# Fixed slots for the pages, moved steps and a three-piece end in a fused Fourier-mixing and gated kernel

## The chip, the cores and the metric

The kernel runs on one core of a Trainium2 chip. The metric is the device time of one execution in microseconds, lower is better. Before the change the median of 3 runs is 802.62 us (801.09 to 804.1).

## The reference

Everything is float32, with S = 2048 positions, D = 512 channels and F = 1792 hidden units.

```python
x = A_x
xn = _layernorm(x, axis=-1)
s = _A_ref(xn, A_dft_seq_re, A_dft_seq_im, A_dft_hid_re, A_dft_hid_im)
g = _silu(_B_ref(xn, B_w_gate, B_w_up, B_w_down))
return x + s * g
```

`_A_ref` multiplies xn by the real and imaginary hidden matrices (512 x 512) to get a and b, then by the sequence matrices (2048 x 2048), and returns Cr a - Ci b. `_B_ref` computes h = sigmoid(xn Wg) * (xn Wu) and returns h Wdown.

## The kernel before

**Products.** Each large product is cut into two-by-two blocks and done in seven block products instead of eight, so that each needs sums and differences of blocks first (`combine`, L128, on VectorE, DVE) and joins of partial results afterwards. Each operand is split into a high part, copied by ScalarE (ACT, L72), and a low part, its difference from the input, by DVE (L73). `mm3` (L75 to L78) then does three matmuls: high x high, high x low, low x high.

**Pages.** All operands, sums and snapshots lie in pages of 4 KB a partition. `page` (L45) asks a pool of 54 slots (`PAGES`, L26) for one, and the pool picks the slot. Whoever first writes a new page waits until everything that read or wrote the slot's former page is done: SyncE (SP) when it is a load (L87, L759), ACT or DVE when it is a split or a sum.

**Order.** The program is a list of units, each with its operands (`needs`) and a function that issues its matmuls. The loop at L1145 walks through it: first come the steps that were placed at this unit by `sooner`, then the loads of the next five units (`LOAD_AHEAD`), then the splits of the next two (`SPLIT_AHEAD`, three for units in `deep`), then the unit itself and the steps placed by `after`. So each engine's order is written out by hand, and each engine works its own queue in that order.

**Stages.** (1) `start` (L495) normalizes and transposes x, and begins the first gate block. (2) Thirteen `block`s (L432) do gate, up and sigmoid for a half of the positions and a group of hidden units; the down products of a block (`Seven`, L359) run during the next one and are added to g_part in HBM by stores from GpSimd (POOL, L312, L315). (3) `seq_units` (L930) multiplies the sequence matrices by xn in four chunks. `PLAN` (L705) writes each chunk's units as a string: a digit is a unit of product 1 to 7 (12 matmuls), a letter a unit of the inner products of a pair of chunks (6 matmuls). In each chunk product 1, 6, 7 and 4 use the chain "a" of two PSUM banks (ga and ua for chunks 0 and 1, gb and ub for 2 and 3, by `LETTER`), 2 the chain "b", 5 and 3 the chain "c" (`CHAIN`, L781). At the end of a product `done` copies a bank pair into a page (`snap`, L809, on ACT) or adds it to one (`join`, L816, on DVE), and `put` (L833) stores it to f_part from POOL. The remaining down products of stage 2 are put between the units after which `LEFT` (L321) names them. (4) `hidden_units` (L962) multiplies by the hidden matrices in two pairs of chunks, applies SiLU to g, multiplies and adds to x in `out`: x is copied there beforehand (`put_x`, L983) and the products are added by POOL's stores.

**Where steps stand.** `CSUM` and `ISUM` say how many units ahead of its use a sum of sequence blocks is made (3 and 4 where nothing is listed), `DEEP` which units split three units ahead, `AL` how early a weight page is loaded and split. `SL`, `GL` and `SI` do the same for sums, splits and SiLU of stage 4, and `LATE`, `S0`, `H0`, `L4`, `S4`, `H4` for the down weights and hidden sums of stage 2.

**The end.** `run_last` (L1075) does the last product in four pieces of columns, d0 256, d1 320 (`CUT`), d0 256, d1 192. Each is multiplied by the gate (L1083), added to x (L1084) and stored; the last is stored in two halves by SP and ACT (L1089).

Of the kernel before, what the change touches and what calls it, by code (L numbers as in the profile page):

```python
# [15 lines left out]
P = 128  # L16
# [6 lines left out]
NT = S // 512  # L23
SB = 512
EPS = 1e-5
PAGES = 54  # L26
SCRATCH = 4096
BLOCKS = (*((0, g) for g in range(1, 7)), (1, 6), *((1, g) for g in range(6)))
FIRST_TURNED = 1, 6
SPLIT_AHEAD = 2  # L30
LOAD_AHEAD = 5


@with_exitstack
def fnet_glu_kernel(ctx: ExitStack, tc: tile.TileContext, x, x_t, c_re, c_im, w_h, w_gu, w_down, out):
# [2 lines left out]

    const = ctx.enter_context(tc.tile_pool(name="const", bufs=1))
    stat = ctx.enter_context(tc.tile_pool(name="stat", bufs=4))  # L40
    pages = ctx.enter_context(tc.tile_pool(name="pages", bufs=PAGES))
    dram = ctx.enter_context(tc.tile_pool(name="dram", bufs=1, space=bass.MemoryType.DRAM))
    banks = ctx.enter_context(tc.tile_pool(name="banks", bufs=1, space=PSUM))

    def page(shape, dtype=F32R):  # L45
        return pages.tile([P, *shape], dtype, name="page")

    def bank(tag):
        return banks.tile([P, 512], F32, name=tag, bufs=2 if tag == "pd" else 1)
# [267 lines left out]

    GATED = {(0, 0): 1, (0, 1): 2, (1, 0): 4, (1, 1): 3}
    SEVEN = (5, 3, 1, 2, 6, 7, 4)
    LATE = 4, 5, 6, 8  # L320
    LEFT = 2, 4, 6, 8, 10, 11, 13  # L321
    HEAD = {(1, 0): "g", (1, 1): "g n u0", (2, 0): "u2", (2, 1): "p1 d0 d1 u1 r", (3, 0): "p3 x1 g d2 u3", (3, 1): "X5 g x2"}
    S0 = 7, 10, 12, 11
    H0 = 8, 11, 13, 14
    L4 = 10, 10, 13, 19
    S4 = 7, 8, 9, 11
    H4 = 8, 10, 11, 12
    SEVEN_LAST = (1, 2, 6, 7, 4, 5, 3)
    waiting = []

# [101 lines left out]
    def block(h, w, made, before, job, late):  # L432

        s, ps = job.s, {}
        n = len(units)
        if not made:
            for i, v in zip((-3, -1, 1, 3), w["s"]):
                sooner(n + i, v.get)

        def snap(k):  # L440
            s[k] = page([2, SB], F32)
            for m, c in enumerate("gu"):
                nc.scalar.activation(s[k][:, m, :], ps[c + "a"], AF.Copy)

        def seed():

            for c in "gu":
                ps[c + "b"] = bank(c + "b")
                nc.scalar.activation(ps[c + "b"], ps[c + "a"], AF.Copy)

        def plus(k):
            for m, c in enumerate("gu"):
                nc.vector.tensor_add(s[k][:, m, :], s[k][:, m, :], ps[c + "c"])

        def gate(k, tag=None):
            if tag:
                s[k] = page([2, SB], F32)
            nc.scalar.activation(s[k][:, 0, :], ps["g" + tag] if tag else s[k][:, 0, :], AF.Sigmoid)

        def times(k, tag=None):  # L460
            nc.vector.tensor_mul(s[k][:, 0, :], s[k][:, 0, :], ps["u" + tag] if tag else s[k][:, 1, :])

        tail = {1: seed, 6: lambda: snap(2), 7: lambda: (snap(3), plus(3)), 3: lambda: plus(2)}
        CH = {1: "a", 5: "c", 2: "b", 6: "a", 7: "a", 4: "a", 3: "c"}

        def unit(k, d):
            first = k in (1, 5)
            for m, c in enumerate("gu"):
                tag = c + CH[k]
                if first:  # L470
                    ps[tag] = bank(tag)
                product(k, ps[tag], w, h, m, first)
            if k in tail:
                tail[k]()
            if d:
                d[0].run(d[1])
            if k in (2, 4):
                gate({2: 1, 4: 4}[k], CH[k])
            if k in (7, 3):
                gate({7: 3, 3: 2}[k])  # L480
            if k == 4:
                times(4, "a")

        for i, k in enumerate((1, 5, 2, 6, 7, 4, 3)):
            if i == 2:
                waiting.extend((before, d) for d in before.items)
            d = waiting.pop(0) if waiting and i in waiting[0][0].at else None
            add([xop[h, k], w[k]] + (d[0].needs(d[1]) if d else []), lambda k=k, d=d: unit(k, d))
        sooner(n + 3, lambda: times(1, "b"))
        sooner(n + 5, lambda: times(3))  # L490
        sooner(n + 7, lambda: times(2))
        job.spread(n, late)
        return job
# [200 lines left out]
    def a_operands():  # L694
# [8 lines left out]
        return ops  # L703

    PLAN = (  # L705
        "111155556666aa33337777b4b444",
        "11ee1f15fc5c5566663gg377773d3d4444",
        "111155556666a7a777b44b443e3e3f3f",
        "1ccg1g1d155d556666337777334444",
    )  # L710
    LETTER = "aabb"
    DEEP = {(0, 1, 3), (0, 5, 3), (0, 6, 3), (0, 7, 3), (0, 4, 3), (1, 1, 3), (1, 5, 3), (1, 7, 3), (1, 4, 3), (3, 6, 3), (2, 4, 0), (2, 6, 3), (3, 4, 1), (3, 7, 3), (0, 7, 1), (3, 7, 0), (2, 7, 2), (0, 6, 0)}
    CSUM = {(0, 7, 1): 5, (2, 6, 0): 4, (2, 6, 1): 5, (1, 6, 0): 2, (3, 4, 2): 3, (1, 5, 1): 5, (2, 6, 3): 3}
    ISUM = {(2, 5, 1): 5, (2, 6, 0): 2, (0, 7, 1): 4, (2, 7, 1): 5, (0, 5, 0): 4, (2, 7, 0): 6}
    AL = {(0, 4, 2): 6, (0, 7, 0): 4, (0, 3, 0): 6, (0, 3, 2): 6, (0, 1, 0): 3, (0, 6, 2): 5, (0, 7, 2): 3}
    INNER_A = 1, 2, 5, 6, 3, 7, 4
    TURNED = (1, 5, 6, 2, 7, 3, 4)

# [211 lines left out]
    def seq_units(job, c_sums):  # L930
        ops = a_operands()
        left = waiting + [(job, k) for k in SEVEN_LAST]
        n = len(units)
        after(n + 40, lambda: nc.scalar.activation(warm, mhalf, AF.Silu))
        for q in range(2):
            sooner(n - (5, 1)[q] - 4, ops[1, q].load)
            sooner(n - (5, 1)[q], ops[1, q].get)
        inner_a([n + i for i in (-45, -38, -37, -36, -34, -31, -27, -24, -16, -10, -4)])
        chunks = [Chunk(i, c_sums) for i in range(NT)]
        starts = []  # L940
        pair = None
        for tc_, plan in enumerate(PLAN):
            starts.append(len(units))
            c = chunks[tc_]
            done = dict.fromkeys(CHAIN, 0)
            for t in plan.replace(" ", ""):
                if t in "abcdefg":
                    if pair is None or pair.ended():
                        pair = Inner(*chunks[tc_ // 2 * 2 :][:2])
                    pair.step("abcdefg".index(t) + 1)  # L950
                    continue
                k = int(t)
                c.step(ops, k, done[k])
                done[k] += 1
                if left and sum(done.values()) in LEFT:
                    last_down(*left.pop(0))
        assert not left
        blocks = [Load(w_h[i, j], [4, D // 2]) for i in range(2) for j in range(2)]
        sums_ahead(diffs, blocks, w_part, [starts[2] + i for i in (2, 8, 11, 16)], 4)


    def hidden_units():  # L962
# [1 line left out]
        v1, v3, v2, v4 = (Load(w_part[i], [4, D // 2]) for i in range(4))  # L964
        a11, a12, a22 = (Load(w_h[i, j], [4, D // 2]) for i, j in ((0, 0), (0, 1), (1, 1)))
        w = {}
        WH = {1: n - 9, 5: n - 8, 6: n - 3}
        for k, v in {1: a11, 5: v1, 6: v2, 2: a12, 7: v3, 3: v4, 4: a22}.items():
            w[k] = Parts([v], v.load, [4, D // 2])
            if k in WH:  # L970
# [1 line left out]
                after(WH[k], w[k].get)  # L972
        CHAIN = {1: "a", 6: "a", 7: "a", 4: "a", 2: "b", 5: "c", 3: "c"}
        BLOCK = {3: (0, 1), 7: (1, 1), 2: (0, 0), 4: (1, 0)}
        LAST, CUT = (NT // 2 - 1, 4), 320

        def place_out(pair, i, t):
            v = out[i * D // 2 : (i + 1) * D // 2, (2 * pair + t) * SB : (2 * pair + t + 1) * SB]
# [10 lines left out]

            return Value([g], make)  # L990

        SI = {(0, 2): 4, (0, 7): 9, (0, 3): 10, (1, 7): 12, (1, 2): 3}
        SL = {(0, 6, 0): 4, (0, 6, 1): 5, (0, 7, 0): 5, (0, 7, 1): 6, (0, 5, 1): 7, (1, 5, 1): 2, (1, 7, 0): 2, (1, 4, 1): 4}
        GL = {(0, 5, 0): 3, (0, 5, 1): 3, (0, 6, 0): 3, (0, 6, 1): 3, (0, 2, 0): 3, (0, 2, 1): 3, (0, 7, 0): 3, (1, 2, 1): 3, (0, 7, 1): 4, (1, 3, 0): 4, (1, 6, 0): 2}
        for pair in range(NT // 2):
            hp = {}
            sums = {}
# [13 lines left out]
            ps, s = {}, {}  # L1011
            for i, k in enumerate(TURNED):
                if k in BLOCK and (pair, k) != LAST:
                    after(n - (88, 84, 79, 77, 72, 67, 60, 60, 56, 68, 64, 58, 54)[i + 6 * pair], lambda pair=pair, k=k: put_x(pair, *BLOCK[k]))

            tags = {"a": ("pd", "b")[pair], "b": "c", "c": "a"}

# [57 lines left out]
            def run_last(k=4, hp=hp, ps=ps, pair=pair, gl=gl, xl=xl):  # L1075
                i, t = BLOCK[k]
                g, xv, r = gl[i, t].get(), xl[i, t].load(), page([2, SB], F32)
                hv, wv = [hp[k, half].get() for half in range(2)], w[k].get()
                for d, at in ((0, slice(0, SB // 2)), (1, slice(0, CUT)), (0, slice(SB // 2, SB)), (1, slice(CUT, SB))):
                    for kt in range(4):  # L1080
                        ws = [v[:, kt, d * P : (d + 1) * P] for v in wv]
                        mm3(ps["a", d][:, at], ws, [v[:, kt % 2, at] for v in hv[kt // 2]], False, kt == 3, go_on=True)
# [1 line left out]
                    nc.vector.tensor_add(r[:, d, at], r[:, d, at], xv[:, d, at])  # L1084
                    row, col = (2 * i + d) * P, (2 * pair + t) * SB
                    to = out[row : row + P, col + at.start : col + at.stop]
                    if (d, at.stop) == (1, SB):
                        for q, rows in ((nc.sync, slice(0, P // 2)), (nc.scalar, slice(P // 2, P))):
                            q.dma_start(to[rows], r[rows, d, at])  # L1089
                    else:  # L1090
# [24 lines left out]
    with tc.manual_schedule():  # L1115
# [15 lines left out]
        n = turned_at  # L1131
        turned_half(12, 0, (n - 19, n - 19, n - 18, n - 12))
        turned_half(19, 1, (n - 12, n - 11, n - 5, n - 5))
        for k, i in {1: -7, 5: -2, 2: -2, 6: 1, 7: 4, 4: 4}.items():
            sooner(n + i, xop[1, k].get)
        for k, i in {1: -4, 2: 0, 3: 1, 4: 2}.items():
            sooner(n + i, lambda k=k: x_sum(1, k))
        xn_sums(0, [n + i for i in (4, 7, 9, 9)])
        xn_sums(1, [n + i for i in (16, 17, 23, 24)])
        c_sums = [Value([], None) for _ in range(4)]  # L1140
        sums_ahead(sums, c_blocks(0, 0), c_sums, [n + i for i in (31, 32, 37, 39)], 3)
        seq_units(job, c_sums)
        hidden_units()
        begin()
# [74 lines left out]
```

## Time and profile before

| | |
|---|---|
| median of 3 runs | 802.62 us (801.09 to 804.1) |
| profiled execution, its own time | 799.84 us |
| its span, first to last instruction | 798.1 us |
| granted TensorE clock, mean | 0.999 |
| data moved by DMA | 172.13 MB, 216 GB/s |

The page of the profile gives each engine's busy time with its share of the span. PE stands for TensorE's matmuls, PEld for its weight loads, which overlap them. A row of the timeline gives a start, a length, the engine, the line of the kernel, the operation, out<-in by tile names, the shape, and in brackets the idle time of that engine just before, with what ended it. The ends of matmuls are modelled, so the distance between two starts tells more of PE than busy time does.

### The profile page before, as it was taken

Reading aid. Unit: us, or ns where it says so; the run is one execution under the profiler, and the core shown is the slowest. Engines: PE = TensorE matmul, PEld = TensorE weight load, DVE = VectorE, ACT = ScalarE, POOL = GpSimd, SP = SyncE. Lnnn points to the kernel's source line nnn. Section 1 sums busy time; section 2 is a strip of 40 time slices with the busy share of each in tenths; the row PEclk is TensorE's granted clock in tenths of the full one; section 3 lists DMA queues with packets and bytes.
Section 4 is the critical chain, followed back from the end, with each engine's and each line's share of the span. In section 5 each row is a group of like instructions: output and inputs, shape, how many; then the busy total and the mean of one; then the engine's idle time right before and its main releaser. Section 6 shows DMA issues by size and latency. Waiting matters only on the chain.

```text
span 798.1 us, 10300 instructions
## 1 busy us (share of the span) xinstructions
PE 790.9 (99%) x3600; PEld 657.7 (82%) x3600; DVE 710.4 (89%) x931; ACT 540.2 (68%) x840; POOL 123.7 (16%) x169
## 2 busy tenths in 40 slices
PE   9999999999999999999999999999999999999997
PEld 7988888888888888888888877888888888888886
DVE  6999899899998989889998887989879899978986
ACT  4688888888877878878977746554444545548371
POOL 2004351111221222112110000000200000000102
PEclk9999999999999999999999999999999999999999
DMA  8048799886897899988998798629949685877836
GB/s 285 32 158 199 177 232 206 194 175 111 170 207 221 215 218 261 256 222 174 218 337 245 166 306 252 225 82 323 410 168 344 229 290 173 301 242 238 193 65 106
DMA packets 49716, 172.13 MB, mean 216 GB/s; under 512 B 5504, under 2 KB 6016, under 8 KB 49664
## 3 DMA queue, kind: packets, MB, share of 16 engines
q0 software_dynamic: 20128, 69.75, 40.7%
q1 hardware_dynamic: 29456, 101.68, 36.0%
q8 instruction: 28, 0.46, 0.2%
q14 instruction: 24, 0.20, 0.1%
q10 hardware_dynamic: 80, 0.05, 0.0%
HBM read 104.86 MB, written 70.26 MB: 219 GB/s over the span
## 4 chain that ended last, share of the span: by engine, by line
PE 96%; DMA 2%; DVE 1%; issue 0%; ACT 0%; DVEq 0%
PE pd L78 6%; PE pd L76 6%; PE pd L77 6%; PE ga L76 6%; PE ga L77 5%; PE ga L78 5%; PE ua L76 5%; PE ua L77 5%; PE ua L78 5%; PE gb L76 4%; PE gb L77 4%; PE gb L78 4%; PE ub L78 4%; PE ub L77 4%; PE ub L76 4%; PE gc L78 3%
## 5 line engine op out<-in xcount | busy, mean ns | idle before, releaser
L73 DVE TENSOR_TENSOR page<-page 128x1024 fp32r<-128x1024 f32 (+2 forms) x408 | 373.9, 943 | 61.4 <-ACT page L72 60.7
L72 ACT ACTIVATE page<-page 128x1024 fp32r<-128x1024 f32 (+2 forms) x408 | 317.5, 832 | 116.3 <-DVE page L128 105.5
L128 DVE TENSOR_TENSOR page<-page 128x512 f32<-128x512 f32 (+2 forms) x280 | 223.1, 817 | 0.9
L310 ACT ACTIVATE page<-pd 128x512 f32<-128x512 f32 x140 | 82.1, 600 | 41.8 <-PE pd L78 38.5
L312 POOL DMA_DIRECT2D g_part<-page x76 | 65.6, 864 | 268.9 <-ACT page L310 252.6
L76 PE MATMUL ga<-page 128*128 128x512 f32 x200 | 78.0, 390 | 1.0 <-DVE page L816 1.0
L77 PE MATMUL ga<-page 128*128 128x512 f32 x200 | 78.0, 390 | 0.0
L78 PE MATMUL pd<-page 128*128 128x512 f32 x200 | 77.9, 390 | 0.0
L76 PE MATMUL pd<-page 128*128 128x512 f32 x200 | 77.8, 389 | 0.0
L78 PE MATMUL ga<-page 128*128 128x512 f32 x200 | 77.8, 389 | 0.0
L77 PE MATMUL pd<-page 128*128 128x512 f32 x200 | 77.8, 389 | 0.0
L76 PE MATMUL ua<-page 128*128 128x512 f32 x196 | 76.3, 389 | 0.0
L77 PE MATMUL ua<-page 128*128 128x512 f32 x196 | 76.3, 389 | 0.0
L78 PE MATMUL ua<-page 128*128 128x512 f32 x196 | 76.2, 389 | 0.0
L76 PE MATMUL gb<-page 128*128 128x512 f32 (+1 forms) x140 | 53.7, 384 | 0.0
L77 PE MATMUL gb<-page 128*128 128x512 f32 (+1 forms) x140 | 53.6, 383 | 0.0
L78 PE MATMUL gb<-page 128*128 128x512 f32 (+1 forms) x140 | 53.6, 383 | 0.0
L77 PE MATMUL ub<-page 128*128 128x512 f32 (+2 forms) x136 | 52.1, 383 | 0.0
L78 PE MATMUL ub<-page 128*128 128x512 f32 (+2 forms) x136 | 52.1, 383 | 0.0
L76 PE MATMUL ub<-page 128*128 128x512 f32 (+2 forms) x136 | 52.1, 383 | 0.0
L76 PE MATMUL gc<-page 128*128 128x512 f32 x124 | 48.3, 389 | 0.0
L78 PE MATMUL gc<-page 128*128 128x512 f32 x124 | 48.2, 389 | 0.0
(156 smaller groups left out, 1298.9 us busy)
## 6 DMA issues: line engine op xcount, KB each, us to landing
g_part<-page POOLq DMA_DIRECT2D x84, 512.0 KB, 6.4
page<-in_c_re_dram SPq DMA_DIRECT2D x49, 512.0 KB, 5.4
page<-in_c_im_dram SPq DMA_DIRECT2D x33, 512.0 KB, 7.2
page<-in_w_gu_dram SPq DMA_DIRECT2D x26, 512.0 KB, 5.6
f_part<-page POOLq DMA_DIRECT2D x16, 512.0 KB, 6.1
page<-f_part SPq DMA_DIRECT2D x16, 512.0 KB, 4.7
page<-i_part SPq DMA_DIRECT2D x14, 512.0 KB, 4.6
page<-in_w_down_dram SPq DMA_DIRECT2D x13, 512.0 KB, 5.0
```

The source lines that it names most:

```text
L72: nc.scalar.activation(hi, src, AF.Copy)
L73: nc.vector.tensor_tensor(lo, src, hi.bitcast(F32), op=SUB)
L76: nc.tensor.matmul(ps, ws[0], ms[0], start=first, stop=False, skip_group_check=go_on)
L77: nc.tensor.matmul(ps, ws[0], ms[1], start=False, stop=False, skip_group_check=go_on)
L78: nc.tensor.matmul(ps, ws[1], ms[0], start=False, stop=last, skip_group_check=go_on)
L128: (engine or nc.vector).tensor_tensor(dst, a, b, op=op)
L310: nc.scalar.activation(pg[:, o, :], po, AF.Copy, scale=float(sign))
L312: nc.gpsimd.dma_start(g_part[i], pg, accum_op=ADD)
```

## The change

The pool of 54 interchangeable slots is replaced by 54 named slots with one buffer each. A string of 1038 letters, `HOMES`, gives the slot of each request for a page, in the order in which they are asked for. The positions of many steps are changed, with the order of units in the four plans. The last product comes in three pieces: d0 256 columns, d1 512, d0 256. What is computed stays as it was.

```diff
-PAGES = 54
+HOMES = (
+    "ab10cdiejfghZYXklmnoqprstuvwxyzABCDEFGHIJ1KLMNOPQ0BRSTUVWcfmqkolzwstAxnJLyZKFuPXcTQYUvMzkIoCtwZyDxEu"
...
+    "zlDKZWtb1uJOjvMXYhIBysaSCdNwlzRgKFDGZ1"
+)
-    pages = ctx.enter_context(tc.tile_pool(name="pages", bufs=PAGES))
+    pages = ctx.enter_context(tc.tile_pool(name="pages", bufs=1))
+    homes = iter(HOMES)
-        return pages.tile([P, *shape], dtype, name="page")
+        return pages.tile([P, *shape], dtype, name="page", tag=next(homes))
-    LATE = 4, 5, 6, 8
-    LEFT = 2, 4, 6, 8, 10, 11, 13
+    LATE = 5, 6, 7, 8
+    LEFT = 2, 4, 7, 9, 10, 11, 12
-    S0 = 7, 10, 12, 11
-    H0 = 8, 11, 13, 14
-    L4 = 10, 10, 13, 19
-    S4 = 7, 8, 9, 11
-    H4 = 8, 10, 11, 12
+    S0 = 7, 9, 12, 10
+    H0 = 8, 11, 12, 11
+    L4 = 10, 12, 15, 19
+    S4 = 9, 7, 8, 9
+    H4 = 8, 9, 12, 11
-            for i, v in zip((-3, -1, 1, 3), w["s"]):
+            for i, v in zip((-2, -1, 1, 2), w["s"]):
-        "111155556666aa33337777b4b444",
-        "11ee1f15fc5c5566663gg377773d3d4444",
-        "111155556666a7a777b44b443e3e3f3f",
-        "1ccg1g1d155d556666337777334444",
+        "1111555566a66a33337777b4b444",
+        "1ee11f15fc555c66663g3g777733d4d444",
+        "111155556666aa7777b44b44e333ef3f",
+        "1ccg1g1d1555d56666337777334444",
-    CSUM = {(0, 7, 1): 5, (2, 6, 0): 4, (2, 6, 1): 5, (1, 6, 0): 2, (3, 4, 2): 3, (1, 5, 1): 5, (2, 6, 3): 3}
+    CSUM = {(0, 7, 1): 5, (2, 6, 0): 4, (2, 6, 1): 5, (1, 6, 0): 2, (3, 4, 2): 3, (1, 5, 1): 5, (2, 6, 3): 5, (2, 5, 0): 2, (3, 4, 3): 4, (2, 7, 1): 3, (1, 6, 1): 3, (3, 7, 0): 5, (3, 7, 2): 2, (3, 5, 1): 3, (2, 4, 2): 4, (1, 5, 0): 3, (3, 7, 1): 3, (2, 7, 2): 4, (2, 5, 2): 3, (2, 4, 0): 2}
...
-        WH = {1: n - 9, 5: n - 8, 6: n - 3}
+        WH = {1: n - 5, 5: n - 4, 6: n - 0}
-        LAST, CUT = (NT // 2 - 1, 4), 320
+        LAST = NT // 2 - 1, 4
-        SI = {(0, 2): 4, (0, 7): 9, (0, 3): 10, (1, 7): 12, (1, 2): 3}
+        SI = {(0, 2): 4, (0, 7): 9, (0, 3): 8, (1, 7): 12, (1, 2): 9, (0, 4): 12, (1, 3): 9, (1, 4): 8}
...
-                    after(n - (88, 84, 79, 77, 72, 67, 60, 60, 56, 68, 64, 58, 54)[i + 6 * pair], lambda pair=pair, k=k: put_x(pair, *BLOCK[k]))
+                    after(n - (94, 79, 81, 81, 75, 67, 55, 64, 62, 65, 64, 66, 58)[i + 6 * pair], lambda pair=pair, k=k: put_x(pair, *BLOCK[k]))
-                for d, at in ((0, slice(0, SB // 2)), (1, slice(0, CUT)), (0, slice(SB // 2, SB)), (1, slice(CUT, SB))):
+                for d, at in ((0, slice(0, SB // 2)), (1, slice(0, SB)), (0, slice(SB // 2, SB))):
-                    if (d, at.stop) == (1, SB):
+                    if (d, at.stop) == (0, SB):
...
```

Left out are the rest of `HOMES` and other positions of the same kind: `DEEP` (18 units before, 22 after), `ISUM`, `AL`, `SL`, `GL`, the inner sums' places and those of the sums of xn and of the weights.

More of the change, by code (lines that the diff above doesn't have):

```diff
@@ L31 @@
 LOAD_AHEAD = 5
+HOMES = (
+    "ab10cdiejfghZYXklmnoqprstuvwxyzABCDEFGHIJ1KLMNOPQ0BRSTUVWcfmqkolzwstAxnJLyZKFuPXcTQYUvMzkIoCtwZyDxEu"
+    "FPVsWc1YUAn0kfMzBZKvyDlEuPsCAQnTckfIMoVBXvy1WtxuElwnT0DcFfIoBCtWZKuvwlPsV0zfXFyAkoCBQvlIwxsMzVXZCoDc"
+    "yQvltfWxnFVzAKPZToCulBftXx0nVAyCidsMPfHlGDcz1jeAIyKQZMONWswDSvRuGCeqmF1rpHiOonKVkWBPfAD0tuyGEMmSdcqp"
+    "KlNnTjzfBrIEMySdDcuGHKlVNizTjAMmnIEcPSdKufzivARjmVMFnH1EpdlBNSuyfzVrTM1KFHEDpNlRfzcuPrMTivBKIDSEjynN"
+    "RmlcAVTSMpKiDqBdnujNlFHRVcMfzEpi1ydmPvjBNrlAnMfzIpiymRNBDqvlHnAFdfiKPpjVERNBcrynFAfGK1PjNEvyxrXzBIFf"
+    "wsADqaVgZGQPMNRclexCdrXJYHoOfjwnsEWgkVpFiGtN0IxeCHYKc1nwOojEsTMWzB0NFkxIcKnuCoOEjwWzBknKcIZoCWudOkBr"
+    "zcXICoTuW1ZBkOSXcsoCfxubhTIBZgdiscULmfxbuoZghsaiW0BlmLJxbouhgiaA0fWBmLbgh0ARBWfQLPghRJAfWLQBRhfALQmR"
+    "BAfsimQdBRfAiPscQdguRBLaAfbi0P1ocJsWuMgRQBCUAahbfLw1PiZm0ocdlWsxgMBQeUAwLP1dfciWlgxBMwL1PicelbBWaM1L"
+    "iPdhecZAmWaMiwLJhd1ZcPumARiMgWLJbCdh0coZmuURgAMisbJdCwc0mZULRPMAWbsaldoJcwB1yvZmPfRgWAasdDlqeJoG1tBx"
+    "uZv0PfVpgWaAQYdHswqlUNyJeFGoME1jtbcxZRBm0rvzhVfaSXWdpHAQnqiwKDPUlCekJOugLbtmTBI0ryhoMvfVpSanQqiwNUPE"
+    "zlDKZWtb1uJOjvMXYhIBysaSCdNwlzRgKFDGZ1"
+)
 @with_exitstack
@@ L705, in fnet_glu_kernel @@
     PLAN = (
-        "111155556666aa33337777b4b444",
-        "11ee1f15fc5c5566663gg377773d3d4444",
-        "111155556666a7a777b44b443e3e3f3f",
-        "1ccg1g1d155d556666337777334444",
+        "1111555566a66a33337777b4b444",
+        "1ee11f15fc555c66663g3g777733d4d444",
+        "111155556666aa7777b44b44e333ef3f",
+        "1ccg1g1d1555d56666337777334444",
     )
     LETTER = "aabb"
-    DEEP = {(0, 1, 3), (0, 5, 3), (0, 6, 3), (0, 7, 3), (0, 4, 3), (1, 1, 3), (1, 5, 3), (1, 7, 3), (1, 4, 3), (3, 6, 3), (2, 4, 0), (2, 6, 3), (3, 4, 1), (3, 7, 3), (0, 7, 1), (3, 7, 0), (2, 7, 2), (0, 6, 0)}
-    CSUM = {(0, 7, 1): 5, (2, 6, 0): 4, (2, 6, 1): 5, (1, 6, 0): 2, (3, 4, 2): 3, (1, 5, 1): 5, (2, 6, 3): 3}
-    ISUM = {(2, 5, 1): 5, (2, 6, 0): 2, (0, 7, 1): 4, (2, 7, 1): 5, (0, 5, 0): 4, (2, 7, 0): 6}
-    AL = {(0, 4, 2): 6, (0, 7, 0): 4, (0, 3, 0): 6, (0, 3, 2): 6, (0, 1, 0): 3, (0, 6, 2): 5, (0, 7, 2): 3}
+    DEEP = {(0, 1, 3), (0, 5, 3), (0, 6, 3), (0, 4, 3), (1, 7, 3), (1, 4, 3), (3, 6, 3), (2, 4, 0), (2, 6, 3), (3, 4, 1), (3, 7, 3), (0, 7, 1), (2, 7, 2), (0, 6, 0), (0, 1, 1), (2, 4, 2), (2, 1, 3), (1, 1, 0), (2, 6, 0), (2, 5, 3), (3, 1, 2), (2, 4, 3)}
+    CSUM = {(0, 7, 1): 5, (2, 6, 0): 4, (2, 6, 1): 5, (1, 6, 0): 2, (3, 4, 2): 3, (1, 5, 1): 5, (2, 6, 3): 5, (2, 5, 0): 2, (3, 4, 3): 4, (2, 7, 1): 3, (1, 6, 1): 3, (3, 7, 0): 5, (3, 7, 2): 2, (3, 5, 1): 3, (2, 4, 2): 4, (1, 5, 0): 3, (3, 7, 1): 3, (2, 7, 2): 4, (2, 5, 2): 3, (2, 4, 0): 2}
+    ISUM = {(2, 5, 1): 4, (2, 6, 0): 4, (0, 7, 1): 5, (2, 7, 1): 5, (0, 5, 0): 4, (2, 7, 0): 6, (2, 6, 1): 4, (2, 4, 1): 4, (0, 6, 1): 3}
+    AL = {(0, 4, 2): 6, (0, 7, 0): 4, (0, 3, 0): 6, (0, 3, 2): 6, (0, 1, 0): 3, (0, 6, 2): 5, (0, 5, 2): 5, (0, 6, 0): 5, (0, 4, 0): 5}
     INNER_A = 1, 2, 5, 6, 3, 7, 4
@@ L935, in seq_units @@
         for q in range(2):
-            sooner(n - (5, 1)[q] - 4, ops[1, q].load)
-            sooner(n - (5, 1)[q], ops[1, q].get)
-        inner_a([n + i for i in (-45, -38, -37, -36, -34, -31, -27, -24, -16, -10, -4)])
+            sooner(n - (6, 4)[q] - 4, ops[1, q].load)
+            sooner(n - (6, 4)[q], ops[1, q].get)
+        inner_a([n + i for i in (-43, -40, -39, -38, -37, -33, -27, -24, -12, -10, 1)])
         chunks = [Chunk(i, c_sums) for i in range(NT)]
@@ L958, in seq_units @@
         blocks = [Load(w_h[i, j], [4, D // 2]) for i in range(2) for j in range(2)]
-        sums_ahead(diffs, blocks, w_part, [starts[2] + i for i in (2, 8, 11, 16)], 4)
+        sums_ahead(diffs, blocks, w_part, [starts[2] + i for i in (3, 9, 10, 14)], 4)
     def hidden_units():
@@ L990, in silu @@
             return Value([g], make)
-        SI = {(0, 2): 4, (0, 7): 9, (0, 3): 10, (1, 7): 12, (1, 2): 3}
-        SL = {(0, 6, 0): 4, (0, 6, 1): 5, (0, 7, 0): 5, (0, 7, 1): 6, (0, 5, 1): 7, (1, 5, 1): 2, (1, 7, 0): 2, (1, 4, 1): 4}
-        GL = {(0, 5, 0): 3, (0, 5, 1): 3, (0, 6, 0): 3, (0, 6, 1): 3, (0, 2, 0): 3, (0, 2, 1): 3, (0, 7, 0): 3, (1, 2, 1): 3, (0, 7, 1): 4, (1, 3, 0): 4, (1, 6, 0): 2}
+        SI = {(0, 2): 4, (0, 7): 9, (0, 3): 8, (1, 7): 12, (1, 2): 9, (0, 4): 12, (1, 3): 9, (1, 4): 8}
+        SL = {(0, 6, 0): 4, (0, 6, 1): 4, (0, 7, 0): 7, (0, 7, 1): 6, (0, 5, 1): 5, (1, 5, 1): 2, (1, 7, 0): 5, (1, 4, 1): 5, (0, 5, 0): 2, (0, 4, 0): 6, (1, 5, 0): 3, (1, 7, 1): 2}
+        GL = {(0, 5, 0): 3, (0, 5, 1): 4, (0, 6, 0): 3, (0, 6, 1): 3, (0, 2, 0): 3, (0, 2, 1): 5, (1, 2, 1): 3, (0, 7, 1): 4, (1, 3, 0): 4, (1, 1, 1): 2, (1, 3, 1): 4, (0, 3, 1): 4, (0, 1, 1): 5}
         for pair in range(NT // 2):
@@ L1133, in fnet_glu_kernel @@
         turned_half(19, 1, (n - 12, n - 11, n - 5, n - 5))
-        for k, i in {1: -7, 5: -2, 2: -2, 6: 1, 7: 4, 4: 4}.items():
+        for k, i in {1: -7, 5: 2, 2: -2, 6: 3, 7: 3, 4: 3}.items():
             sooner(n + i, xop[1, k].get)
-        for k, i in {1: -4, 2: 0, 3: 1, 4: 2}.items():
+        for k, i in {1: -6, 2: -2, 3: 0, 4: 2}.items():
             sooner(n + i, lambda k=k: x_sum(1, k))
-        xn_sums(0, [n + i for i in (4, 7, 9, 9)])
-        xn_sums(1, [n + i for i in (16, 17, 23, 24)])
+        xn_sums(0, [n + i for i in (3, 6, 10, 12)])
+        xn_sums(1, [n + i for i in (15, 16, 24, 25)])
         c_sums = [Value([], None) for _ in range(4)]
-        sums_ahead(sums, c_blocks(0, 0), c_sums, [n + i for i in (31, 32, 37, 39)], 3)
+        sums_ahead(sums, c_blocks(0, 0), c_sums, [n + i for i in (30, 32, 37, 39)], 3)
         seq_units(job, c_sums)
```

## The prediction, as it was written before the result was known

> **What bounds it.** I read the page first, then the busy time by stretches, then the table of waits, then the timeline at the few places where TensorE (PE) stood still. The page says that PE is never far from busy, and that the chain of work that ended last is almost all PE.
>
> ```profile
> span 798.1 us, 10300 instructions
> PE 790.9 (99%) x3600; PEld 657.7 (82%) x3600; DVE 710.4 (89%) x931; ACT 540.2 (68%) x840; POOL 123.7 (16%) x169
> PE 96%; DMA 2%; DVE 1%; issue 0%; ACT 0%; DVEq 0%
> ```
>
> Busy time overstates a pipelined engine, so the next view counts matmuls per stretch (columns: stretch and its length, then busy time and number of instructions of PE, weight loads, DVE, ACT, POOL, granted clock, DMA share, GB/s).
>
> ```profile
> 200.00:400.00 200.00, 200.00 (x884) 165.62 (x883) 179.28 (x292) 162.94 (x295) 43.06 (x57) 1.00 0.90 218
> 440.00:480.00 40.00, 38.98 (x172) 31.90 (x171) 34.70 (x36) 25.58 (x32) 2.82 (x4) 1.00 0.82 242
> 480.00:520.00 40.00, 39.99 (x175) 32.36 (x174) 34.52 (x33) 22.77 (x28) 2.93 (x4) 1.00 0.74 235
> 560.00:600.00 40.00, 40.00 (x178) 33.13 (x177) 33.16 (x30) 19.61 (x24) 3.94 (x7) 1.00 0.73 292
> 640.00:680.00 40.00, 40.00 (x178) 33.14 (x177) 39.42 (x39) 19.87 (x21) 1.60 (x3) 1.00 0.67 233
> ```
>
> A matmul lasts 0.39 us in the records, so some two of each count straddle an edge. 882 in 200 us are 0.227 us each, and 176 in 40 us are 0.227 us too. That is the pace of one 128x512 matmul that waits for nothing. Only 440 to 480 and 480 to 520 fall short, by six and by three: 6 x 0.227 = 1.4 us and 3 x 0.227 = 0.7 us, each to within one matmul. So about 2 of 798 us in the middle are waiting, and the rest is matmuls that the change keeps. This caps the gain. The waits of PE itself, in the table of waits (total, times, longest), name the largest:
>
> ```profile
> PE ga L76 <- DVE page L816: 1.0, 1, 1.0
> ```
>
> Here is that place on PE's timeline, and DVE's, ACT's and POOL's just ahead of it.
>
> ```profile
> 470.81 0.39 PE L77 MATMUL ub<-page 128*128 128x512 f32 x1
> 471.04 0.39 PE L78 MATMUL ub<-page 128*128 128x512 f32 x1
> 472.44 0.47 PE L76 MATMUL ga<-page 128*128 128x512 f32 x1 [1.02 <-DVE page L816]
> 472.75 0.40 PE L77 MATMUL ga<-page 128*128 128x512 f32 x1
> ...
> 461.40 6.04 DVE L73 TENSOR_TENSOR page<-page 128x1024 fp32r<-128x1024 f32 x7
> 469.33 2.36 DVE L73 TENSOR_TENSOR page<-page 128x1024 fp32r<-128x1024 f32 x2 [1.89 <-ACT page L72]
> 471.61 0.68 DVE L816 TENSOR_TENSOR page<-ga,page 128x512 f32<-128x512 f32 x1
> ...
> 468.24 2.01 ACT L72 ACTIVATE page<-page 128x1024 fp32r<-128x1024 f32 x2 [2.37 <-DMA f_part<-page]
> ...
> 460.65 0.56 POOL L833 DMA_DIRECT2D f_part<-page  x1 [7.64 <-DVE page L816]
> ```
>
> Read from the bottom: the store to f_part was issued at 460.65. ACT waited 2.37 us, to 468.24, for it to land, since its split (L72) was to write into the slot that the store still read. DVE, whose L73 follows that split, idled 1.89 us; the join L816, behind it in DVE's order, came late; and PE, which had to wait until L816 had read bank ga, started 472.44 - 471.04 - 0.227 = 1.17 us late, and the next matmul 0.31 - 0.227 = 0.08 us late. That is 1.25 us from a slot given too early. It is what a fixed table can mend.
>
> **The change.** *The work.* The diff adds and drops no operand, product or transfer; each chunk's plan holds the same digits and letters in another order. So L72, L73, L128 and every load and store stay as many, and DVE's 710.4 us stay. I cost them at nothing because PE's 0.227 us steps hide them; the cover is DVE's idle time, thin in one place: 40 - 39.42 = 0.58 us between 640 and 680.
>
> *The table.* 1038 letters name 54 slots, as many as PAGES was, so no memory is gained. If the split at 468.24 gets a free slot, DVE's two L73 start 1.89 us sooner, at 467.44, and end at 469.80. What is late next is L816, which must wait for PE's last write of its banks, and PE's six inner matmuls (ub) stand between; L816 on ga would end near 470.5 and PE is due at 471.04 + 0.227 = 471.27. Nothing is left of the wait: -1.25 us. Bounds: 0 if that slot or an equal one is late again, -1.25 if not; I take -1.25, as the row shows the one releaser.
>
> *Moved steps.* Two other pauses lie in the short stretches:
>
> ```profile
> 484.56 0.39 PE L78 MATMUL ua<-page 128*128 128x512 f32 x1
> 484.95 0.50 PE L76 MATMUL ga<-page 128*128 128x512 f32 x1
> 485.29 0.40 PE L77 MATMUL ga<-page 128*128 128x512 f32 x1
> ...
> 494.62 0.39 PE L76 MATMUL ga<-page 128*128 128x512 f32 x1
> 494.96 0.50 PE L77 MATMUL ga<-page 128*128 128x512 f32 x1
> 495.30 0.40 PE L78 MATMUL ga<-page 128*128 128x512 f32 x1
> ```
>
> At 485 it is (0.39 - 0.227) + (0.34 - 0.227) = 0.28 us, where chunk 0 ends with product 4 in banks ga and ua and chunk 1 begins with product 1 in the same banks. Both plans keep that, and so does this pause. At 495 it is 0.11 + 0.11 = 0.22 us, inside the first products of chunk 1, where the plan goes from 11ee1f15 to 1ee11f15, so other splits stand there: bounds 0 and -0.22, I take -0.2, the row itself. The other moves (sums one to three units sooner or later, splits at depth three, hidden weights three or four units later, the gate's SiLU up to ten units sooner) put a load on SP's queue and a page in use earlier or later. Below I bound what they can cost together.
>
> *The end in three pieces.* Rows of the old end, with PE's chain giving a 320-column step and the list of DMA issues the landing:
>
> ```profile
> 789.30 0.15 PE ub L76
> ...
> 792.21 0.28 PE L78 MATMUL gb<-page 128*128 128x256 f32 x1
> 792.33 0.25 PE L76 MATMUL ub<-page 128*128 128x192 f32 x1
> 792.53 0.42 DVE L1083 TENSOR_TENSOR page<-page,gb 128x256 f32<-128x256 f32 x1 [0.43 <-PE gb L78]
> 792.99 0.42 DVE L1084 TENSOR_TENSOR page<-page 128x256 f32<-128x256 f32 x1
> 793.54 0.27 PE L78 MATMUL ub<-page 128*128 128x192 f32 x1
> 793.85 0.35 DVE L1083 TENSOR_TENSOR page<-page,ub 128x192 f32<-128x192 f32 x1 [0.44 <-PE ub L78]
> 794.24 0.36 DVE L1084 TENSOR_TENSOR page<-page 128x192 f32<-128x192 f32 x1
> ...
> out_dram<-page SPq DMA_DIRECT2D x2, 128.0 KB, 3.1
> out_dram<-page SPq DMA_DIRECT2D x1, 48.0 KB, 2.1
> ```
>
> A 192-column step is (793.54 - 792.33) / 11 = 0.11 us. Twelve steps each of 320 and 192 columns become twelve of 512: 12 x (0.15 + 0.11 - 0.227) = 0.4 us off PE. The last pair of DVE operations is 256 wide instead of 192: (792.99 - 792.53 + 0.42) - (794.24 - 793.85 + 0.36) = +0.13 us. The last DMAs grow from 48 to 64 KB each: between 0 and 3.1 - 2.1 = 1.0 us, I take +0.05, since 64 lies nearest to 48. The middle piece needs two 512-wide DVE operations, 2 x 0.68 = 1.36 us by the L816 row, under the 12 x 0.12 = 1.44 us of the last piece; that cover is thin, but what slips past it is under 0.2 us. Sum of the end: -0.2 us, bounds -0.3 and +0.9.
>
> *The sum.* -1.25 - 0.2 - 0.2 = -1.65 us. The profiled execution took 799.84 us (its span of 798.1 and 1.7 us around it), so it becomes 798.2 us. The median of the runs shown is 802.62, or 2.78 us above the profiled one. I take the sum off the median: 801.0 us.
>
> **Rivals.** *Late slots (slower).* SP issues every load in one order, and a load whose slot is not free holds all behind it. From its queue's waits and the list of waits:
>
> ```profile
> SPq L87 <- DVE page L73: 144.6, 39, 16.5
> ACT page L72 <- DMA page<-s_part: 0.4, 1, 0.4
> DMA to landing us min/median/max: 2.9/6.1/10.0
> ```
>
> SP already waits 144.6 us in 39 waits for DVE's last readers, yet past the head ACT and DVE wait only 0.4 us in all for a load: the loads come early enough. The third row, for the f_part stores, spans 7.1 us from the shortest to the longest, and a table fixed beforehand can't follow that. Counted in the diff, 45 of the 1038 requests take a slot last given 12 requests before or less, and 35 of them stand in one run, requests 624 to 727, near the stretches that already fall short. A 2.37 us wait there cost PE 1.25 us. Four new ones cost 5.0 us and leave 802.62 - 1.65 + 5.0 = 806.0; eight leave 811.0. It decides from the second such wait on, which eats up the gain. For it: most slots are taken the moment they are free. Against it: the median distance in the table is 28 requests.
>
> *More than the profile shows (faster).* If the 2.78 us between the profiled run and the median are waits of the same kind, and the table ends those too, the result is 802.62 - 1.65 - 2.78 = 798.2. For it: these runs differ with the work unchanged. Against it: no trace shows those waits.
>
> *The change does not do what it says.* The pause at 472 goes and another slot is late as often: only the end's -0.2 is left, 802.4.
>
> *Another pace.* The table moves pages to other addresses; if operands' places set the 0.227 us, one ns on each of the page's 3600 matmuls is 3.6 us either way. The stretches speak against it: the same 0.227 at DMA shares of 0.67 to 0.90 and in every stage. The Trainium skill (TensorE: Matmul & The Clock Gate, section Back-to-back issue gap) gives N / 2.4 + 2.5 ns, 216 ns at 512 columns; by it some 11 ns a matmul would be lost here, 40 us in all, to be won or not by placement. The trace does not agree with that figure.
>
> **The numbers.** A measurement of this kernel can tell about 0.5% from no change: under 798.6 is faster, over 806.6 slower. My forecast, 799 to 803 around 801.0, gets 0.50; it is the only case whose releaser a row names. No effect, 802.4: 0.12. More than the profile shows, 798.2: 0.15, of which 0.11 lies under 798.6. Late slots, 804 to 813: 0.21, of which 0.16 lies over 806.6. Another pace: 0.02, half on each side. That makes faster 0.12, slower 0.17 and the same 0.71. The range runs from 798.0 to 807.6: below it are 0.05 of the third case, above it 0.13 of the late slots, and the pace's 0.02. It contains the end's bounds and the zero bound of each wait.
>
> **Signs.** Right: the count in 440 to 480 rises from 172 toward 178, no ACT L72 waits for an f_part store ahead of a join, the 0.28 us where chunk 1 begins is still there, and the last matmul is 256 wide with some 0.4 us less of PE from the start of the last product. Wrong: ACT or DVE rows that wait for page loads or stores by more than 2 us with PE late behind them, fewer than 176 matmuls in a stretch that has 178 now, or DVE with no idle time at all between 640 and 680 and PE late there. It would be quite wrong if full-width matmuls came at another pace than 0.227 us.

## The result, and the profile after

The changed kernel takes 797.75 us (median of 6 runs, 797.66 to 798.25) against 802.71 us of the kernel before (6 runs beside it, 801.09 to 804.1). The ratio is 0.9942, 95% interval 0.9929 to 0.9955. In a later set on one chip it was 797.82 us against 800.63 us, ratio 0.9959, interval 0.9947 to 0.9971. So the changed kernel's own time stays within 0.1 us between these two sets, while the kernel before gave medians of 802.71, 801.01, 800.63 and 800.42 us in four sets. The gain is 0.4 to 0.6%, about the 0.5% that the prediction set for "faster", and the time lies 0.25 us below the predicted range. One run of `y2_one_slot` below took 992.16 us at a granted clock of 0.753, against 0.996 or more in every other run whose clock is known, and is left out of its comparison.

The two profiled executions are closer than the medians: 797.77 us after, 799.84 us before. The page of after:

```profile
span 796.0 us, 10261 instructions
PE 789.9 (99%) x3588; PEld 657.3 (83%) x3588; DVE 711.3 (89%) x929; ACT 542.5 (68%) x840; POOL 119.6 (15%) x169
PE 99%; DVE 0%; ACT 0%; issue 0%
```

The chain that ended last no longer passes through a DMA (2% before). Busy time by stretches, after:

```profile
200.00:400.00 200.00, 200.00 (x884) 165.66 (x883) 181.12 (x293) 163.77 (x295) 42.53 (x56) 1.00 0.92 219
440.00:480.00 40.00, 40.00 (x178) 33.01 (x177) 36.50 (x38) 26.52 (x33) 2.82 (x4) 1.00 0.84 261
480.00:520.00 40.00, 39.99 (x177) 32.67 (x176) 34.88 (x34) 23.89 (x31) 2.91 (x4) 1.00 0.73 229
640.00:680.00 40.00, 40.00 (x178) 33.12 (x177) 39.68 (x39) 20.96 (x22) 1.60 (x3) 1.00 0.66 250
```

The count from 440 to 480 rose from 172 to 178, the undisturbed number, and from 480 to 520 from 175 to 177. DVE is as full as before from 640 to 680, and PE does not notice. The only PE pause left after the first 35 us is the one that both plans keep, at the start of chunk 1 (timeline of PE, after):

```profile
483.13 0.39 PE L92 MATMUL ua<-page 128*128 128x512 f32 x1
483.53 0.50 PE L90 MATMUL ga<-page 128*128 128x512 f32 x1
483.86 0.39 PE L91 MATMUL ga<-page 128*128 128x512 f32 x1
```

It is (0.40 - 0.227) + (0.33 - 0.227) = 0.28 us, as before. The clearest difference is in the table of waits. ACT's and DVE's waits of over 1 us in total for a DMA, first before, then after (total, times, longest):

```profile
ACT page L507 <- DMA page<-in_w_gu_dram: 5.8, 2, 4.2
ACT page L72 <- DMA g_part<-page: 2.5, 3, 1.8
ACT page L72 <- DMA f_part<-page: 2.4, 1, 2.4
DVE stats L172 <- DMA page<-in_x_dram: 2.4, 2, 2.0
```

```profile
ACT page L521 <- DMA page<-in_w_gu_dram: 4.8, 2, 3.9
DVE stats L186 <- DMA page<-in_x_dram: 2.2, 1, 2.2
```

A name with `<-page` on its right is a store that still reads a slot. Before, ACT waited for four such stores, 4.9 us in all; after, for none. What remains are waits for loads from the inputs x and w_gu.

### The profile page after: what moved, and what is told of

Read it like the earlier page. It is cut to its first block, busy times and chain, and to the rows that moved or that the text cites. A ratio compares the mean times of both kernels' runs of the same rounds, so it can differ in the third digit from the quotient of the medians.

```text
span 796.0 us, 10261 instructions
## 1 busy us (share of the span) xinstructions
PE 789.9 (99%) x3588; PEld 657.3 (83%) x3588; DVE 711.3 (89%) x929; ACT 542.5 (68%) x840; POOL 119.6 (15%) x169
## 4 chain that ended last, share of the span: by engine, by line
PE 99%; DVE 0%; ACT 0%; issue 0%
PE ga L90 6%; PE pd L90 6%; PE ga L91 6%; PE ga L92 6%; PE pd L91 6%; PE pd L92 6%; PE ua L90 6%; PE ua L91 6%; PE ua L92 6%; PE gb L91 4%; PE gb L90 4%; PE gb L92 4%; PE ub L91 4%; PE ub L90 4%; PE ub L92 4%; PE gc L90 4%
## 5 line engine op out<-in xcount | busy, mean ns | idle before, releaser
L87 DVE TENSOR_TENSOR page<-page 128x1024 fp32r<-128x1024 f32 (+2 forms) x408 | 372.4, 945 | 53.2 <-ACT page L86 52.2
L142 DVE TENSOR_TENSOR page<-page 128x512 f32<-128x512 f32 (+2 forms) x280 | 224.5, 820 | 1.3
L90 PE MATMUL ub<-page 128*128 128x512 f32 x132 | 51.4, 389 | 0.0
L91 PE MATMUL ub<-page 128*128 128x512 f32 x132 | 51.4, 389 | 0.0
L92 PE MATMUL ub<-page 128*128 128x512 f32 x132 | 51.3, 389 | 0.0
```

The source lines that it names most:

```text
L87: nc.vector.tensor_tensor(lo, src, hi.bitcast(F32), op=SUB)
L90: nc.tensor.matmul(ps, ws[0], ms[0], start=first, stop=False, skip_group_check=go_on)
L91: nc.tensor.matmul(ps, ws[0], ms[1], start=False, stop=False, skip_group_check=go_on)
L92: nc.tensor.matmul(ps, ws[1], ms[0], start=False, stop=last, skip_group_check=go_on)
L142: (engine or nc.vector).tensor_tensor(dst, a, b, op=op)
```

## The experiments

Each set names the time of the kernel before beside it.

**The pool's choice with the moved steps** (`x1_pool_choice`, set with 801.01 us before):

```diff
-    pages = ctx.enter_context(tc.tile_pool(name="pages", bufs=1))
+    pages = ctx.enter_context(tc.tile_pool(name="pages", bufs=54))
-        return pages.tile([P, *shape], dtype, name="page", tag=next(homes))
+        return pages.tile([P, *shape], dtype, name="page")
```

> The changed kernel with its moved steps and its three-piece end, but with the pool of 54 slots choosing again. If the fixed table makes the gain (theory A: waits for slots that differ from run to run), most of the 5.0 us comes back: 800.5 to 803 us, and the profile has splits or joins that wait for a store or a late reader with PE late behind them. If the moved steps make it (theory B: other orders of units and other leads give the engines room), it stays at 797.7 to 798.7 us.

Measured: 799.9 us (798.27 to 800.56), ratio 0.9987, interval 0.9976 to 0.9998. Neither theory alone: about 1.1 us of gain stays without the table, some 2 us of it are gone, and the runs spread over 2.3 us, where the changed kernel's spread over 0.6. Its profiled execution, at 798.27 us, is one of the two shortest of the twelve and has hardly more pauses than after's (0.44 us after the first 35 us, against 0.28); what the longer runs waited for was not seen. The slots were tight, though: worked out from each page's first writer and its slot's last user, 19 pages that ACT or DVE write first begin within 2 us after a store out of their slot has landed in this trace, and four in after's.

**The pool's own slots as a table** (`x2_own_table`, same set):

```diff
+HOMES = (...the slots that the pool chose...)
-    pages = ctx.enter_context(tc.tile_pool(name="pages", bufs=PAGES))
+    pages = ctx.enter_context(tc.tile_pool(name="pages", bufs=1))
+    homes = iter(HOMES)
-        return pages.tile([P, *shape], dtype, name="page")
+        return pages.tile([P, *shape], dtype, name="page", tag=next(homes))
```

> The kernel before with the very slots that its pool chose, written out as a table. Theories A and B both expect no change, 802.7 us within 0.7, since no page moves. A third theory C, that naming a slot for each request makes other waits than a pool does, expects 798 to 801 us. Its profile is a second look at an execution of before's order: if waits differ from run to run, it shows pauses that the first profile does not have, up to 3 us of them.

Measured: 800.76 us, ratio 1.0, interval 0.9987 to 1.0013. Naming slots costs and gains nothing that this interval, about 1 us to either side, could tell. Its profile is a second trace of before's order. ACT, DVE, POOL and PE at the place of the first profile's largest pause:

```profile
468.78 1.06 ACT L87 ACTIVATE page<-page 128x1024 fp32r<-128x1024 f32 x1 [2.54 <-DMA f_part<-page]
...
469.87 2.36 DVE L88 TENSOR_TENSOR page<-page 128x1024 fp32r<-128x1024 f32 x2 [2.02 <-ACT page L87]
...
461.06 0.56 POOL L848 DMA_DIRECT2D f_part<-page  x1 [7.64 <-DVE page L831]
...
471.40 0.39 PE L93 MATMUL ub<-page 128*128 128x512 f32 x1
472.98 0.47 PE L91 MATMUL ga<-page 128*128 128x512 f32 x1 [1.20 <-DVE page L831]
```

The same chain, and PE now loses 1.58 - 0.227 = 1.35 us on this matmul, where it lost 1.17 us.

**The kernel before with another table** (`x3_planned_table`, same set). The letters are worked out from the first profile's times by the rule in the expectation; against x2 only they differ.

```diff
-HOMES = (...the slots that the pool chose...)
+HOMES = (...the slots by the rule...)
```

> The kernel before, nothing moved and the old end, with a table of my own: from the first profile, each page that ACT or DVE writes first gets the slot last freed among those free for 2 us or more (6 us after a store from POOL), each load the slot freed last. Theory A: the table alone ends most waits, 798.5 to 800.5 us. Theory B: 802 to 803 us, because the order of the steps still leaves ACT and DVE late.

Measured: 798.68 us (798.33 to 799.71), ratio 0.9973, interval 0.9963 to 0.9983. The table alone gives 2.3 us with the steps where they were, as theory A expected, and the twelve runs spread over 1.4 us where x2's twelve spread over 2.1. In its table of waits ACT and DVE wait for no store; the longest two of their waits for a DMA are for loads:

```profile
ACT page L522 <- DMA page<-in_w_gu_dram: 5.4, 2, 4.3
DVE stats L187 <- DMA page<-in_x_dram: 2.0, 1, 2.0
```

**The three-piece end alone** (`x4_end_only`, same set):

```diff
-        LAST, CUT = (NT // 2 - 1, 4), 320
+        LAST = NT // 2 - 1, 4
-                for d, at in ((0, slice(0, SB // 2)), (1, slice(0, CUT)), (0, slice(SB // 2, SB)), (1, slice(CUT, SB))):
+                for d, at in ((0, slice(0, SB // 2)), (1, slice(0, SB)), (0, slice(SB // 2, SB))):
-                    if (d, at.stop) == (1, SB):
+                    if (d, at.stop) == (0, SB):
```

> The kernel before with the last product in three pieces and nothing else. By the prediction -0.2 us. By the two profiles, in which the last product takes 10.36 us to the span's end both times, 0.0 us: PE ends 0.35 us sooner, DVE takes 0.13 us longer, and the larger last DMAs take the rest back. Neither can be told from 802.7 us in the times; the profile's distance from the first 256-wide matmul to the end of the span decides.

Measured: 800.88 us, ratio 0.9993, interval 0.9981 to 1.0006. From the first matmul of the last product to the end of the span its profile has 10.36 us, as before's has, and after's 10.35. It is also a third trace of before's order of steps: the store to f_part landed later still, and PE lost more.

```profile
469.03 1.06 ACT L72 ACTIVATE page<-page 128x1024 fp32r<-128x1024 f32 x1 [3.08 <-DMA f_part<-page]
...
471.12 0.39 PE L78 MATMUL ub<-page 128*128 128x512 f32 x1
473.23 0.47 PE L76 MATMUL ga<-page 128*128 128x512 f32 x1 [1.73 <-DVE page L816]
```

Here it is 2.11 - 0.227 = 1.88 us. ACT's waits of 2.37, 2.54 and 3.08 us went with 1.17, 1.35 and 1.88 us of PE: 0.71 us more of waiting, 0.71 us more of pause. In these three traces PE paid in full for what that store kept ACT waiting longer.

**The changed kernel again** (`y1_after_again`, set with 800.63 us before), no edit.

> The changed kernel once more, beside the three that follow and the kernel before. Every theory expects about 5 us under the kernel before where that has 802.7 us, and about 3 us under it where that has 801.0 us: 797.7 to 798.3 us, its runs within 0.6 us of each other. Were the first comparison's 5 us a matter of that chip alone, it would be 799 us or more.

Measured: 797.82 us (797.66 to 798.1), ratio 0.9959, interval 0.9947 to 0.9971, as expected.

**One slot exchanged** (`y2_one_slot`, same set). The table is that of x2; from the waiting split's request on, two of the 54 letters change places, so that 31 of the 1038 letters differ.

```diff
-HOMES = (...the slots that the pool chose...)
+HOMES = (...the same, two slots exchanged from request 628 on...)
```

> The kernel before with its own slots as a table, but two of the 54 slots change places from one request on: the split that waits for the f_part store at 468 us gets a slot free 4.3 us earlier, and the store's slot goes to a low part needed 2.2 us later. Theory A: the pause of 1.25 us (1.4 and 1.9 us in the two later profiles of the same order) is gone from the profile, and the time falls by 1.2 to 2.0 us. If something else holds DVE there, the pause stays and the time too.

Measured: 799.4 us, ratio 0.998, interval 0.9969 to 0.999: 1.2 us, at the lower end of what was expected. DVE and PE at the old place:

```profile
465.90 4.76 DVE L88 TENSOR_TENSOR page<-page 128x512 fp32r<-128x512 f32 x6
470.58 0.68 DVE L831 TENSOR_TENSOR page<-ga,page 128x512 f32<-128x512 f32 x1
...
471.86 0.39 PE L93 MATMUL ub<-page 128*128 128x512 f32 x1
472.08 0.39 PE L91 MATMUL ga<-page 128*128 128x512 f32 x1
```

DVE no longer idles ahead of the join, and the matmul on ga starts 0.22 us after the one before it. One exchange of two slots is worth 1.2 of the 2.8 us that the whole change gives in this set. Its profile also has a pause of 0.37 us at 454.5 that the first profile lacks: there ACT waited 0.9 us for a load from s_part, ahead of the exchange.

**The changed kernel with my table** (`y3_after_replanned`, same set).

```diff
-HOMES = (...the change's letters...)
+HOMES = (...letters by the rule of x3, from after's profile...)
```

> The changed kernel's steps and end with a table of my own, made by the same rule from its profile: no page that ACT or DVE writes first takes a slot within 2 us of a store's landing (four do in the changed kernel's own table). If keeping stores' slots away is what the table does, it is as fast as the changed kernel, 797.4 to 798.0 us. If the letters hold something more, such as places that suit the operands, it is slower by over 0.5 us.

Measured: 798.38 us (797.95 to 798.79), ratio 0.9966. It misses its range by 0.4 us: the change's own table is better than mine by 0.56 us, just past the 0.5 us by which the expectation would say that the letters hold something more. My table's profile has no wait of ACT or DVE for a store either, but the pause at the start of chunk 1 is 0.62 us instead of 0.28, with ACT's copy (L823) beginning 0.3 us late (PE's timeline):

```profile
483.65 0.39 PE L92 MATMUL ua<-page 128*128 128x512 f32 x1
484.38 0.50 PE L90 MATMUL ga<-page 128*128 128x512 f32 x1 [0.34 <-ACT page L823]
```

The rows name no releaser of that copy but PE itself, and the slot that it writes had been free for 2.4 us, so why it is late stays open. Places that suit the operands are not the reason: the pace from 200 to 400 us is 0.227 us with either table.

**An adverse table** (`y4_adverse_table`, same set).

```diff
-HOMES = (...the change's letters...)
+HOMES = (...letters by the opposite rule, from after's profile...)
```

> The changed kernel's steps and end with a table made by the opposite rule: by the profile's own times no wait is needed, but ACT's and DVE's new pages take, wherever one is free, the slot that a POOL store has left last; 91 of them stand within 1 us of a store's landing, two in the changed kernel's table. Theory A: the stores land at other times in each run, so waits come up, the time is 799.5 to 804 us, and the runs lie 1.5 us or more apart. Theory B, that the steps' places carry the gain: under 798.5 us.

Measured: 802.18 us (800.78 to 803.55), ratio 1.0017, interval 1.0008 to 1.0027: slower than the kernel before, with every moved step in place, and spread over 2.8 us, as theory A expected. ACT's and DVE's waits for stores, the six largest:

```profile
ACT page L86 <- DMA f_part<-page: 5.9, 2, 4.7
...
ACT page L86 <- DMA g_part<-page: 3.7, 3, 2.0
ACT page L324 <- DMA g_part<-page: 3.7, 4, 2.0
ACT page L472 <- DMA g_part<-page: 3.5, 3, 1.6
DVE page L87 <- DMA g_part<-page: 2.8, 3, 1.6
...
DVE page L142 <- DMA i_part<-page: 1.7, 1, 1.7
```

These are 21.3 us in 16 waits, of which PE felt part. Its pauses after the first 35 us sum to 3.0 us in this profile, against 0.28 in after's. Three of them, at 96, 125 and 751 us, 1.6 us together, lead back to an ACT or DVE instruction that began within 0.11 us after a store had landed out of the very slot that it writes. The second of them, on ACT's and PE's timelines:

```profile
122.55 1.06 ACT L86 ACTIVATE page<-page 128x1024 fp32r<-128x1024 f32 x1 [1.99 <-DMA g_part<-page]
...
124.62 0.39 PE L92 MATMUL uc<-page 128*128 128x512 f32 x1
125.14 0.50 PE L90 MATMUL pd<-page 128*128 128x512 f32 x1
```

For the rest no store is shown, and the same letters made slots that readers other than stores leave tighter as well, so not all of the 4.4 us over y1 need be stores.

**The last pause** (`z1_boundary`, set with 800.42 us before): an attempt at a version faster than both.

```diff
-        "1ee11f15fc555c66663g3g777733d4d444",
+        "e1e11f15fc555c66663g3g777733d4d444",
-    "zcXICoTuW1ZBkOSXcsoCfxubhTIBZgdiscULmfxbuoZghsaiW0BlmLJxbouhgiaA0fWBmLbgh0ARBWfQLPghRJAfWLQBRhfALQmR"
+    "zcXICoTuW1ZBkOSXcsoCfxubhTIBdZgiscfLmUxbuoZaisghW0BlJmLbxouhgiaA0fWBmLbgh0ARBWfQLPghRJAfWLQBRhfALQmR"
```

> The changed kernel, with chunk 1 begun by an inner unit (6 matmuls in another bank) ahead of its first product unit, and the letters of the table moved along with their requests. The pause of 0.28 us at the start of chunk 1, where PE waits for ACT to copy banks ga and ua, should go, since the inner unit's 1.36 us cover the copy: 797.5 us, or 0.3 us under the changed kernel. If the splits for the inner unit come late instead, the pause moves there and the time is 797.8 to 798.3 us.

Measured: 798.49 us (798.1 to 798.68), ratio 0.9974. It is slower than the changed kernel in the other sets. The pause at the start of chunk 1 is gone, and one of 0.57 us stands in a unit before it (PE's timeline):

```profile
478.43 0.39 PE L90 MATMUL ga<-page 128*128 128x512 f32 x1
479.11 0.50 PE L91 MATMUL ga<-page 128*128 128x512 f32 x1 [0.29 <-DVE page L87]
479.45 0.40 PE L92 MATMUL ga<-page 128*128 128x512 f32 x1
```

DVE's low part (L87) comes late there; on DVE's timeline two sums (L142, 2.36 us together) stand just ahead of it, at 475.57. That moving the inner unit ahead brought them there is argued, not shown. The expectation had named the case, but the time lies 0.2 us over the range that it gave.

**The old end in the changed kernel** (`z2_old_end`, same set):

```diff
-        LAST = NT // 2 - 1, 4
+        LAST, CUT = (NT // 2 - 1, 4), 320
-                for d, at in ((0, slice(0, SB // 2)), (1, slice(0, SB)), (0, slice(SB // 2, SB))):
+                for d, at in ((0, slice(0, SB // 2)), (1, slice(0, CUT)), (0, slice(SB // 2, SB)), (1, slice(CUT, SB))):
-                    if (d, at.stop) == (0, SB):
+                    if (d, at.stop) == (1, SB):
```

> The changed kernel with the old end in four pieces, the last 192 wide. The prediction's term for the three pieces, -0.2 us, makes this one 798.0 us; the profiles' 10.36 us from the last product's start to the end of the span, with either end, make it 797.8 us, the same as the changed kernel within 0.1 us.

Measured: 798.02 us (797.84 to 798.6), ratio 0.9965, interval 0.9949 to 0.998. The time is that of the first case, 0.2 us over the changed kernel's medians of other sets. The profile is that of the second: 10.35 us from the last product to the end of the span, as with three pieces. By the profile the end is worth nothing; by the times, which come from different sets, up to 0.2 us can't be excluded.

## Why the prediction was right and wrong

**What bounds the kernel.** Right. PE's pace is unchanged (882 matmuls in 200 us again), and the gain is waiting taken out. In the twelve traces PE's pauses after the first 35 us (steps between full-width matmuls beyond 0.227 us) sum to 0.28 us in the changed kernel, 2.00 in the kernel before and 2.99 with the adverse table, and each execution's time less its pauses is 797.5 to 798.2 us.

**The table, -1.25 us.** Right in place and mechanism: the pause is gone, y2 takes it away with one exchange, and three traces tie its length to the landing of one store. Its size was that of a lucky execution: the profiled run of before took 799.84 us, less than all six timed runs beside it, and in the two later traces the matmul alone lost 1.35 and 1.88 us.

**The moved steps, -0.2 us at 495; 0.28 us kept at 485.** Both right. Beyond them two small pauses of 0.13 and 0.11 us, at 615 and 750, and some 0.14 us ahead of the first full-width matmul are gone, on which the prediction had no term; the last also varies by 0.6 us among the profiles. x1 puts the moved steps with the pool's choice at 1.1 us.

**The end, -0.2 us.** The mis-sized term is the last DMA, taken at +0.05 us. PE did lose 0.35 us and DVE took 0.13 us longer, but the rest of the tail came up 0.2 us. The issue before, then the last DVE operations and the issue after, on the timeline; and the last two DMAs in the list of issues (size and time to landing), first before, then after:

```profile
794.63 0.54 SPq L1089 DMA_DIRECT2D out_dram<-page  x1
...
791.45 0.42 DVE L1097 TENSOR_TENSOR page<-page,gb 128x256 f32<-128x256 f32 x1
791.91 0.43 DVE L1098 TENSOR_TENSOR page<-page 128x256 f32<-128x256 f32 x1
792.36 0.54 SPq L1103 DMA_DIRECT2D out_dram<-page  x1
```

```profile
out_dram<-page SPq DMA_DIRECT2D x1, 48.0 KB, 2.1
out_dram<-page ACTq DMA_DIRECT2D x1, 48.0 KB, 2.3
...
out_dram<-page SPq DMA_DIRECT2D x1, 64.0 KB, 2.2
out_dram<-page ACTq DMA_DIRECT2D x1, 64.0 KB, 2.5
```

From the issue to the end of the span it is 798.06 - 794.63 = 3.4 us before and 796.0 - 792.36 = 3.6 us after. With bounds of 0 and 1.0 us, the smallest value near the lower one was too kind.

**The sum and the median.** This is the step that failed. The prediction took -1.65 us off the median of 802.62 us, and so left the 2.78 us between the profiled run and the median as if the change could not touch them. The changed kernel shows no such gap: its profiled run took 797.77 us and its median is 797.75. The rival "more than the profile shows" had priced this at 798.2 us, 0.45 us from the result, with a chance of 0.15. The case against it, that no trace shows those waits, was weak, since runs of one program lay 3 us apart. x2 and x4 show the same pause longer, and x3 and the changed kernel, which have no such wait, run within 1.4 and 0.6 us. That all of the 2.78 us were waits of this kind is not shown. In the later sets the kernel before took 800.4 to 801.0 us, 0.6 to 1.2 us over the first profiled run, and no execution of over 801 us was traced: by the sum above, one of 802.6 us would need 4.4 to 5.1 us of pauses, where no trace shows over 3.0, or another cause.

**Late slots.** Real as a mechanism, wrong for this table. The adverse table did what this rival said, at 4.4 us. Its row of landings from 2.9 to 10.0 us was misread: those are sixteen different stores, and in the three traces of before's order each of them landed in the same time within 1.8 us, so a table can allow for a store that is slow. What spoke for the rival, 45 short distances in the string (with a median of 29 requests, not 28), measured nothing: worked out from each page's first writer and its slot's last user, 17 pages that ACT or DVE write first stood within 2 us after a store's landing before, four after. The distance that counts is in time and from a store, not in requests.

**Another pace.** Did not happen: the table puts pages into other slots and the pace is 0.227 us still. So the figure of 216 ns for 512 columns, which the Trainium skill (TensorE: Matmul & The Clock Gate, section Back-to-back issue gap) gives for an isolated matmul, does not appear here with either placement, nor does the 131 ns that it gives for a stream. Another hint of the Trainium skill (Perfetto Trace Analysis, section Optimization Strategy), that repeated bubbles can mean too little memory for the next tile, bears on this case with a twist that the runs show: 54 slots were enough, and which of them was taken made the bubble.

## What to carry to other kernels

Where slots are taken again and again, look in the table of waits for ACT or DVE waiting for a store out of a page, and give a page that a compute engine writes first a slot that no store has just left; loads, issued early, can take those. Compare the profiled run with the spread of the timed runs before trusting the length of any wait in it: a spread of 0.4% on unchanged work can come from waits, and may be part of what a change takes away. A shorter last product buys nothing when the last operations and the last transfer grow with it.

## What was not expected of the hardware

The time of the kernel before varied by 3 us over six runs (801.09 to 804.1) and by 5.5 us over 35 runs on one chip (798.76 to 804.26). Over twelve runs each, its steps varied by 2.1 and 3.0 us with the pool's slots (x2, x4) and by 1.4 us with a table that keeps stores' slots away (x3). The changed kernel's steps varied by 2.3 us with the pool's slots (x1), by 2.8 us with the adverse table (y4), and by 0.4 to 0.6 us over six runs with the change's own. So much of the variation goes with the choice of slots.

The granted clock may have a share in the longest runs. The three later sets hold 70 runs of the kernel before. All ten of them that took over 802.5 us show a clock of 0.996 to 0.998, while the 56 at 0.999 or 1.0 stay under 802.2 us. None of the long ones was traced, so whether longer waits lowered the clock or a lower clock made the runs longer stays open. It does not carry the gain: those 56 runs have a mean of 800.5 us, still 2.7 us over the changed kernel, whose runs at 0.998 took 797.66 to 797.81 us.
